# Turns and numerators of a linear-attention front as pairs of 64-row matmuls, with the front's order made anew

## The chip, the cores and the metric

The kernel runs on one core of a Trainium2 chip. A core has five engines with an instruction queue each: TensorE (PE, matmuls into PSUM; its weight loads are shown as PEld), VectorE (DVE), ScalarE (ACT), GpSimd (POOL) and SyncE (SP). Each works through its queue in order. Transfers between HBM and the on-chip SBUF go over 16 DMA engines; SP and POOL issue them here, and each of the two has a DMA queue of its own. The metric is device microseconds of one execution, as the median of several runs. A matmul takes a stationary operand (`lhsT`, up to 128 rows by 128 columns) and a moving one (`rhs`); a turn (transpose) is a matmul with an identity matrix.

## The reference

A linear attention over 8 batches, 8 heads, 576 tokens, head size 64, followed by a mixture of 8 experts with Sinkhorn-normalised gates:

```python
q_p, k_p = (phi(q), phi(k))              # phi(x) = (x if x > 0 else exp(x) - 1) + 1
kv = np.einsum('bhsd,bhse->bhde', k_p, v)
z = np.sum(k_p, axis=2)
num = np.einsum('bhsd,bhde->bhse', q_p, kv)
den = np.einsum('bhsd,bhd->bhs', q_p, z)[..., None] + 1e-06
x = num / den                            # then laid out as (4608 tokens, 512)
logits = x @ w_gate; P = exp(logits - max); 8 rounds of row and column normalisation
for e in range(8):
    out += P[:, e:e + 1] * (np.maximum(x @ w1[e], 0.0) @ w2[e])
```

## The kernel before

**Stages.** The front makes `xT`, the attention output with features on the partitions, in fp16. The experts follow: hidden activations `h`, then outputs `ye`, gated and added into `acc`. For expert 0 the first five groups of 512 tokens are plain matmuls (hidden: L626, 32 matmuls of 128x512 a group; output: L894, 32 of them); they are the work with which TensorE fills the front. Later units use a seven-product scheme, with sums of `x`, of weights and of `h` made on DVE. Sinkhorn runs on DVE behind the front.

**A block of the front** is `att(b, g)`: one batch and four heads, 16 blocks numbered n = 2b + g. Heads stand in two pairs: `hh` picks the 64 partitions on which a head of a pair lies, `r` the pair. Tokens of a batch are split as partition w (64) and j (9). The steps of a block, with the profile's lines:

- loads of k, q and v (L293), by SP for blocks 0, 1 and 6 to 15, by POOL for blocks 2 to 5 and for v from block 6 on (then with a cast to fp16). k and q share a tile `kqin` of which there are two, so k of block n + 2 waits for the last reader of k and q of block n;
- ACT: exp of k and of q (L309); DVE: `t` = max(x + 1, 1) (L322), then min with exp (L325), for k and q each; v is copied into `vv` (L260 on DVE, L258 on ACT), beside a column of ones;
- TensorE L354: k'v and k's sum over the 9 values of j, as 18 matmuls with a contraction of 64 rows each, in pairs (`hh` = 0 and 1) that lie on the two halves of the array and write two PSUM banks;
- `kvz` (L368 on DVE, L366 on ACT): the result goes to SBUF in fp16, multiplied by a mask (`diag` or `half_`) that leaves only the blocks of one head each;
- TensorE L384: 9 turns of q, 128x128 each, both heads of a pair at once; copied to `qpT` (L260, L258);
- TensorE L410: numerators and denominators, 10 matmuls of 128 rows with 130 moving columns: 6 and then 4. The mask in `kvz` lets one matmul do two heads;
- denominators plus 1e-6 (L422 on DVE, L420 on ACT), reciprocal (L425), product `xn` (L434 on DVE, L431 on ACT);
- TensorE L449: 10 turns of x, 128x128 each; copied to `xT` (L260, L258).

`logits(b2)` (L470) is 36 matmuls of 8 columns for two batches. At the start TensorE runs 34 warm-up matmuls (L544) between its first tasks.

**Order.** `_Plan` collects tasks with engines, durations and dependences. `order`, a list of task numbers by engine at the end of the kernel, fixes the sequence in which each engine's tasks are emitted, and so its queue. An engine that waits for one task holds up all that stand behind it in its list. In the list of the DMA engines a number stands only for a landing; the transfers themselves move in the order of the queue that issued them.

**Weights.** `load_w1` and `load_w2` issue the expert's weights on POOL (L243), for expert 0 in two parts each. The first part of w1 waits for the gate copy (L345), which waits for v of block 0. POOL's list of before begins: identity, gate copy, w1 part 1 and 2, k, q, v of block 2, k, q, v of block 3, w2 part 1 and 2, k and q of block 4.

DVE's list of before has, at the same place: the `xT` copies of block 0, the denominators, reciprocals and `xn` of block 1, its `xT` copy, and then L322 for k and q of block 2.

Of the kernel before, what the change touches and what calls it, by code (L numbers as in the profile page):

```python
# [10 lines left out]
FP32 = mybir.dt.float32  # L11
FP16 = mybir.dt.float16
# [127 lines left out]
def kernel(  # L140
# [64 lines left out]
    diag = fp.tile([P, 2, D + 1], FP16, tag="diag", name="diag", bufs=1)  # L205
    half_ = fp.tile([P, 2], FP32, tag="half", name="half", bufs=1)
    p_kv = S_.pool(2)

    def bank_tile():
        return hqp.tile([P, 1024], FP16, tag="hq", name="hq")  # L210

# [63 lines left out]
    def att(b, g):  # L275
# [82 lines left out]
        tkv = fadd(("pe", 0.54), f_kv, deps=[tph["k"], *tvv, *kv_id[n - 1:n], *(num_id[n - 2] if n > 1 else [])], acq=[gkv],  # L358
                   use=[gvv, gt["k"]], prio=pr)

        def f_z(e):
            gz["tile"] = fp.tile([P, 2, 2, D + 1], FP16, tag="kvz", name="kvz")
            kv_ = gkv["tile"][:, :, 0:2 * (D + 1)].rearrange("p h (r d) -> p h r d", r=2)
            if e == "act":
                for r in range(2):
                    nc.scalar.mul(out=gz["tile"][:, :, r, :], in_=kv_[:, :, r, :], mul=half_[:, r:r + 1])  # L366
            else:
                nc.vector.tensor_tensor(out=gz["tile"], in0=kv_,  # L368
                                        in1=diag[:, None, :, :].broadcast_to([P, 2, 2, D + 1]), op=ALU.mult)
        tz = [fadd({"dve": 0.42, "act": 0.63}, f_z, deps=[tkv], acq=[gz], use=[gkv], prio=pr)]  # L370
# [6 lines left out]
        for j0, j1 in ((0, 5), (5, NJ)) if n < 2 else ((0, NJ),):  # L377
            gp = S_.grp(p_hq if n < 2 else p_kv)

            def f_qt(_, gp=gp, j0=j0, j1=j1):  # L380
                tl = bank_tile() if n < 2 else pair_tile(FP16).rearrange("p b t -> p (b t)")
                gp["tile"] = tl[:, 0:(j1 - j0) * 2 * PW].rearrange("p (j h w) -> p j h w", h=2, w=PW)
                for j in range(j0, j1):
                    nc.tensor.transpose(gp["tile"][:, j - j0].rearrange("p h w -> p (h w)"),  # L384
                                        gt["q"]["tile"][:, j, 2:4, :].rearrange("p r d -> p (r d)"), ident)

            def f_qc(e, gp=gp, j0=j0, j1=j1):
                copy(e, gq["tile"][:, :, j0:j1, :].rearrange("p h j w -> p j h w"), gp["tile"])
            t1 = fadd(("pe", 0.058 * (j1 - j0)), f_qt, deps=[tph["q"], tqa, t_init], acq=[gp], use=[gt["q"]], prio=pr)
            tq.append(fadd({"act": 0.165 + 0.105 * (j1 - j0), "dve": 0.14 + 0.069 * (j1 - j0)}, f_qc, deps=[t1, tqa],  # L390
                           use=[gp, gq], prio=pr))
# [4 lines left out]
        def f_xa(_):  # L396
            gxn["tile"] = fp.tile([P, 5, 2, 2, D], FP16, tag="xn", name="xn")
# [3 lines left out]
        for i0, i1 in ((0, 3), (3, 5)):  # L401
# [3 lines left out]
            def f_num(_, i0=i0, i1=i1, gn=gn, grd=grd):  # L405
                gn["tile"] = pair_tile()
                grd["tile"] = fp.tile([P, 2, 6], FP32, tag="rden", name="rden", bufs=4)
                for i in range(i0, i1):
                    for hh in range(2):
                        nc.tensor.matmul(gn["tile"][:, hh, 2 * D1 * (i - i0):2 * D1 * (i - i0 + 1)],  # L410
                                         lhsT=gq["tile"][:, hh, js[i]:js[i] + 2, :].rearrange("p j w -> p (j w)"),
                                         rhs=gz["tile"][:, hh].rearrange("p r e -> p (r e)"), start=True, stop=True)

            def num(gn=gn, ni=ni):
                return gn["tile"][:, :, 0:2 * D1 * ni].rearrange("p h (m e) -> p h m e", e=D1)
# [11 lines left out]
            def f_xn(eng, num=num, grd=grd, i0=i0, i1=i1, ni=ni):  # L427
                if eng == "act":
                    for m in range(2 * ni):
                        for h in range(2):  # L430
                            nc.scalar.mul(out=gxn["tile"][:, i0 + m // 2, m % 2, h, :], in_=num()[:, h, m, 0:D],  # L431
                                          mul=grd["tile"][:, h, m:m + 1])
                    return
                nc.vector.tensor_tensor(  # L434
                    out=gxn["tile"][:, i0:i1].rearrange("p i r h e -> p h (i r) e"), in0=num()[:, :, :, 0:D],
                    in1=grd["tile"][:, :, 0:2 * ni, None].broadcast_to([P, 2, 2 * ni, D]), op=ALU.mult)
            t1 = fadd(("pe", 0.12 * ni), f_num, deps=tq + tz + [txa], acq=[gn, grd], use=[gq, gz], prio=pr)
# [4 lines left out]
        for c0, c1 in ((0, 1), (1, 2)) if n < 2 else ((0, 2),):  # L442
            gx = S_.grp(p_hq if n == 0 else p_kv)

            def f_xt(_, gx=gx, c0=c0, c1=c1):
                gx["tile"] = bank_tile()[:, None, :] if n == 0 else pair_tile(FP16)[:, 0:c1 - c0]
                for c2 in range(c0, c1):
                    for i in range(5):
                        nc.tensor.transpose(gx["tile"][:, c2 - c0, 64 * js[i]:64 * js[i] + P],  # L449
                                            gxn["tile"][:, i, c2].rearrange("p h e -> p (h e)"), ident)  # L450

            def f_xc(e, gx=gx, c0=c0, c1=c1):
                copy(e, xT[:, 2 * g + c0:2 * g + c1, S * b:S * b + S], gx["tile"][:, :, 0:S])
            t1 = fadd(("pe", 0.28 * (c1 - c0)), f_xt, deps=txn, acq=[gx], use=[gxn], prio=pr)
            t1 = fadd({"act": 0.11 + 0.53 * (c1 - c0), "dve": 0.04 + 0.42 * (c1 - c0)}, f_xc, deps=[t1], use=[gx], prio=pr)
            for c2 in range(c0, c1):
                xt_done[(b, 2 * g + c2)] = t1
# [5 lines left out]
    def logits(b2):  # L463
# [11 lines left out]
        t1 = lg_pe[b2] = fadd(("pe", 1.0), f_l, deps=[xt_done[(b, c)] for b in (2 * b2, 2 * b2 + 1) for c in range(NDT)],  # L475
# [78 lines left out]
    nc.vector.memset(diag, 0.0)  # L554
    nc.vector.memset(half_, 0.0)
    for i in range(2):
        nc.vector.memset(vv_t[i][:, :, :, D], 1.0)
        nc.vector.memset(diag[64 * i:64 * i + 64, i, :], 1.0)
        nc.vector.memset(half_[64 * i:64 * i + 64, i:i + 1], 1.0)
# [43 lines left out]
    def layer1(e, g):  # L603
        gw1, tw1, gw2, tw2 = w_t[e]
        bs = range(512 * g // S, (512 * g + 511) // S + 1)
        xd_ = [xt_done[(b, c)] for b in bs for c in range(NDT)]
# [10 lines left out]
        for f, c0, c1 in jobs:  # L617
# [13 lines left out]
            t1 = add(("pe", 0.2175 * (c1 - c0)), f_hq, deps=[tw1[f // 4], prev_hq[0]] + xd_[0:c1 if g == 0 else None],  # L631
# [9 lines left out]
    def x_blocks(g):  # L641
        bs = range(512 * g // S, (512 * g + 511) // S + 1)
        deps = [xt_done[(b, c)] for b in bs for c in range(NDT)]
# [205 lines left out]
    def out_dma(g, tt, deps, c0=0, cw=DM):  # L849
        def f_o(_):  # L850
            for half in range(2):
                bb, j = divmod(2 * (4 * g + tt) + half, NJ)
                dst = AP(tensor=out.tensor, offset=(S * bb + j) * DM + c0, ap=[[NJ * DM, PW], [1, cw]])
# [276 lines left out]
    for d, k_ in zip(chain, chain[1:]):  # L1130
# [3 lines left out]
        pool 0 50 106 108 110 112 114 140 142 144 171 173 177 179 544 181 207 209 211 241 271 303 333 363 393 425 455  # L1134
        485 515 525 576 573 1561 1081 1570 1563 1572 1574 1565 1109 1107 1083 1567 1230 1206 1576 1204 1232 1327 1329
        1353 1355
        pe 2 3 4 5 6 7 8 9 10 11 12 13 14 15 16 17 18 56 54 19 51 20 21 22 63 59 23 24 25 88 90 26 27 85 28 29 67 69
        97 93 614 615 30 616 31 32 33 101 103 34 35 617 618 620 622 624 626 127 628 124 630 632 134 157 154 130 164
        638 636 160 138 637 639 168 640 641 651 653 194 191 634 175 197 655 635 224 657 221 201 659 227 661 663 231
        673 665 205 251 671 254 235 674 672 284 261 684 281 686 688 257 291 690 667 287 668 265 692 669 295 316 694  # L1140
        313 346 670 343 297 323 696 353 700 349 698 319 717 706 719 376 701 373 721 327 357 723 707 403 383 725 379
        702 727 406 729 438 704 387 435 705 409 413 731 703 750 441 752 417 739 445 733 465 740 498 495 734 468 501
        735 505 754 449 756 509 758 471 737 419 475 738 529 526 760 479 532 762 536 764 736 540 770 771 542 768 571
        769 766 794 808 810 796 798 767 800 802 814 772 804 816 818 812 806 547 773 846 820 848 852 850 860 854 826
        856 550 864 866 862 827 858 868 828 898 829 553 904 902 870 900 822 823 556 824 872 908 825 906 912 880 559
        914 916 910 918 878 881 920 922 950 876 562 956 952 879 924 954 874 875 958 877 960 964 565 926 970 962 966
        968 974 1014 1016 972 976 1020 928 1022 1018 1024 929 927 1026 1028 568 1030 932 1034 1036 1032 930 1038 1042
        1044 931 1040 1048 1050 1046 933 1052 982 980 1054 1056 981 1058 1062 983 1064 1060 1066 1137 1139 978 1068
        1143 984 979 985 1145 1141 1074 1076 1079 1147 1084 1087 1149 1151 1153 1090 1157 1159 1155 1161 1165 1167
# [77 lines left out]
```

## Time and profile before

| what | value |
|---|---|
| median of 3 runs | 954.46 us (953.85 to 954.76) |
| the profiled execution's span | 952.4 us |
| TensorE | 943.2 us busy in 7092 matmuls, clock 1.00 |
| front (L470 of the last two batches) | ends near 121.8 us |
| loads of k, q by SP | 576 KB each |
| weight loads of POOL | 512 KB in SBUF for a half of expert 0's w1 or w2 |

How to read it: the span runs from the first to the last instruction; the median of the runs is taken around the whole execution. Times in the trace count from the span's start. A group "x18" is a merged row of 18 instructions. A matmul's own duration (219 ns for a 128-column turn) is its passage through the array; the next one starts earlier, and what a matmul costs is the distance from start to start (56 ns there).

### The profile page before, as it was taken

The page shows a single profiled execution, that of the slowest core. Times are in us where ns is not written, and L with a number is a line of the kernel's source. Part 1 is how long each engine was busy: PE and PEld are TensorE (multiplying, and loading weights), DVE is VectorE, ACT ScalarE, POOL GpSimd, SP SyncE. Part 2 cuts the span into 40 slices and gives each one's busy share as a digit, 9 for nine tenths or more (in the row PEclk, how much of TensorE's full clock was granted, in tenths as well). Part 3 has the DMA queues.
Part 4 walks back from the last instruction along what each step waited for, and adds up shares of the span by engine and source line. Part 5 has one row for each costly group of instructions (what it writes and reads, how often), then busy time and mean ns, then how long its engine had stood idle before and what let it go on. Part 6 is the DMA issues. An engine that isn't in the chain of part 4 may idle for free.

```text
span 952.4 us, 18434 instructions
## 1 busy us (share of the span) xinstructions
PE 943.2 (99%) x7092; PEld 643.9 (68%) x7092; DVE 771.0 (81%) x1527; ACT 566.6 (59%) x1030; POOL 161.5 (17%) x209
## 2 busy tenths in 40 slices
PE   8999999999999999999999999999999999999998
PEld 4566676466676667766676666766676666766676
DVE  6999998788887787888887787887877788877776
ACT  6799755665555555555555555555555555555551
POOL 4210100012122211221112211221112211111111
PEclk9999999999999999999999999999999999999999
DMA  9989983253255422544145431644125431425545
GB/s 310 326 247 255 217 251 115 48 98 89 67 150 112 111 67 61 112 111 100 57 128 116 93 96 43 137 111 101 57 73 105 110 95 56 139 78 151 153 113 133
DMA packets 109944, 118.85 MB, mean 125 GB/s; under 512 B 7840, under 2 KB 95520, under 8 KB 109856
## 3 DMA queue, kind: packets, MB, share of 16 engines
q1 hardware_dynamic: 81600, 90.33, 31.1%
q0 software_dynamic: 27856, 26.82, 16.5%
q8 instruction: 55, 0.90, 0.4%
q10 hardware_dynamic: 400, 0.52, 0.2%
q14 instruction: 33, 0.27, 0.1%
HBM read 119.69 MB, written 17.69 MB: 144 GB/s over the span
## 4 chain that ended last, share of the span: by engine, by line
PE 96%; DMA 2%; DVE 1%; SPq 0%; ACT 0%; POOL 0%; issue 0%; POOLq 0%
PE ye L1032 34%; PE hq L772 20%; PE att L772 10%; PE ye L894 7%; PE Zye L1032 6%; PE Zye L772 5%; PE hq L777 4%; PE hq L626 3%; PE att L777 2%; DMA kqin<-in_k_dram 2%; PE Zye L777 1%; PE kv_ps L354 1%; PE kv_ps L449 1%; PE kv_ps L410 1%; PE kv_ps L384 1%; PE kv_ps L470 0%
## 5 line engine op out<-in xcount | busy, mean ns | idle before, releaser
L1046 DVE SCALAR_TENSOR_TENSOR acc<-ye,P_sb,acc 128x256 f32<-128x256 f32 x620 | 266.8, 476 | 103.7 <-PE ye L1032 101.6
L1032 PEld LDWEIGHTS <-S 128*128 128x128 f16 x1984 | 194.1, 98 | 45.9 <-issue 0.2
L1056 POOL TENSOR_TENSOR acc<-acc,h 128x256 f32<-128x256 f32 x124 | 103.0, 848 | 603.3 <-ACT h L1053 603.3
L1032 PE MATMUL ye<-h,S 128*128 128x256 f16 x1488 | 192.8, 273 | 0.0
L1032 PEld LDWEIGHTS <-h 128*128 128x128 f16 x1488 | 145.6, 98 | 39.9
L812 ACT ACTIVATE h<-hq 128x512 f16<-128x512 f32 x134 | 80.1, 598 | 136.3 <-PE hq L772 117.6
L772 PEld LDWEIGHTS <-W 128*128 128x128 f16 x896 | 87.7, 98 | 81.0 <-issue 0.2
L772 PE MATMUL hq<-xs,W 128*128 128x512 f16 x448 | 133.2, 379 | 0.0
L772 PE MATMUL att<-xs,W 128*128 128x512 f16 x448 | 133.2, 379 | 0.0
L772 PE MATMUL hq<-xs,w 128*128 128x512 f16 x448 | 124.1, 379 | 0.0
L772 PEld LDWEIGHTS <-w 128*128 128x128 f16 x672 | 65.8, 98 | 54.8
L815 DVE CUSTOM_DVE_ANT_0 h<-att,s 128x512 f16<-128x512 f32 x126 | 86.4, 685 | 20.3 <-ACT s L799 19.9
L809 ACT ACTIVATE h<-Zye 128x512 f16<-128x512 f32 x134 | 80.2, 599 | 31.8 <-PE Zye L772 27.3
L1053 ACT ACTIVATE h<-Zye,P_sb 128x256 f32<-128x256 f32 x124 | 52.5, 471 | 77.7 <-PE Zye L1032 75.6
L792 ACT COPY Zye<-hq 128x512 f32<-128x512 f32 x134 | 77.7, 580 | 31.7 <-PE hq L772 25.0
L815 DVE CUSTOM_DVE_ANT_0 h<-hq,s 128x512 f16<-128x512 f32 x126 | 86.3, 685 | 12.4 <-PE hq L772 11.8
L799 ACT COPY s<-hq 128x512 f32<-128x512 f32 x126 | 73.6, 584 | 34.2 <-PE hq L772 29.9
L1003 DVE TENSOR_TENSOR S<-h 128x1024 f16<-128x1024 f16 x124 | 85.0, 685 | 5.5 <-ACT h L812 5.5
L806 ACT COPY s<-att 128x512 f32<-128x512 f32 x126 | 74.5, 591 | 1.2 <-PE hq L777 0.7
L894 PE MATMUL ye<-w,h 128*128 128x512 f16 x296 | 73.7, 379 | 0.0
L772 PE MATMUL Zye<-xs,w 128*128 128x512 f16 x224 | 66.6, 379 | 0.0
L1032 PE MATMUL ye<-w,h 128*128 128x256 f16 x496 | 64.3, 273 | 0.0
(129 smaller groups left out, 1078.3 us busy)
## 6 DMA issues: line engine op xcount, KB each, us to landing
xs<-xd SPq DMA_DIRECT2D x196, 256.0 KB, 4.1
w<-in_moe_w_dram POOLq DMA_DIRECT2D x48, 256.0 KB, 4.2
out_dram<-acc SPq DMA_DIRECT2D x67, 128.0 KB, 2.4
kqin<-in_k_dram SPq DMA_DIRECT2D x12, 576.0 KB, 4.3
kqin<-in_q_dram SPq DMA_DIRECT2D x12, 576.0 KB, 6.1
xs<-xd SPq DMA_DIRECT2D x49, 128.0 KB, 2.3
xd<-xT SPq DMA_DIRECT2D x27, 128.0 KB, 3.8
vin<-in_v_dram POOLq DMA_DIRECT2D x10, 288.0 KB, 5.9
```

The lines of the kernel that those rows point to most:

```text
L772: nc.tensor.matmul(dst, lhsT=lhs(0, c), rhs=X(b)(c), start=(first and c == 0), stop=(c == 1), skip_group_check=True)
L792: nc.scalar.copy(out=Zt[1], in_=gX["tile"])
L799: nc.scalar.copy(out=gs2["tile"], in_=gX["tile"])
L806: nc.scalar.copy(out=gs5["tile"], in_=gR["tile"])
L809: nc.scalar.activation(out=hd(0, 0), in_=Zt[1], func=AF.Relu)
L812: nc.scalar.activation(out=hd(1, 0), in_=gX["tile"], func=AF.Relu)
L815: nc.vector._custom_dve(TENSOR_ADD_SAT, out=dst, in0=ps, in1=sb, s0=3.0e38, s1=0.0)
L894: nc.tensor.matmul(gy[tt]["tile"], lhsT=hx(f, P * tt, P), rhs=gw2["tile"][:, f, :], start=(f == 0), stop=(f == NFT - 1))
L1003: nc.vector.tensor_tensor(out=gS[i]["tile"], in0=a0, in1=a1, op=op)
L1032: nc.tensor.matmul(bank(g_)[:, s, :], lhsT=lhs(s, kk), rhs=rhs(kk), start=(new and s == 0 and kk == 0), stop=(kk == 3), skip_group_check=True)
L1046: nc.vector.scalar_tensor_tensor(out=dst(), in0=bank(g_)[:, s, :], scalar=P_sb[:, gg, e:e + 1], in1=dst(), op0=ALU.mult, op1=ALU.add)
L1056: nc.gpsimd.tensor_tensor(out=dst(), in0=dst(), in1=gst["tile"], op=ALU.add)
```

## The change

- q is turned by 18 matmuls of 64 rows (`turn`), one for each head, in pairs on the halves of the array. The two halves write two PSUM banks, so that each bank holds one `hh`. The copies to `qpT` are cut by bank for blocks 0 and 1.
- The numerators of the two heads of a pair are matmuls of 64 rows and 65 columns, again as pairs on two banks: 20 for a block in place of 10. So the mask in `kvz` falls away, with `diag`, `half_` and their memsets; `kvz` becomes a plain copy.
- x is turned by 18 matmuls of 64 rows; the even and the odd j of a batch go to two banks, and the copies to `xT` are cut into one of 2 x 256 and one of 2 x 320 columns. The tokens of a batch stand in another order in `xT` (j = 0, 2, 4, 6 and then 1, 3, 5, 7, 8), and `out_dma` maps the output rows accordingly.
- The dependences follow (two copies behind each `xT` part), the plan's durations too, and every list in `order` is replaced.

```diff
+    def turn(dst, src, h):
+        r_ = slice(64 * h, 64 * h + 64)
+        nc.tensor.transpose(dst, src[r_], ident[r_, r_])
...
-            kv_ = gkv["tile"][:, :, 0:2 * (D + 1)].rearrange("p h (r d) -> p h r d", r=2)
-            if e == "act":
-                for r in range(2):
-                    nc.scalar.mul(out=gz["tile"][:, :, r, :], in_=kv_[:, :, r, :], mul=half_[:, r:r + 1])
-            else:
-                nc.vector.tensor_tensor(out=gz["tile"], in0=kv_,
-                                        in1=diag[:, None, :, :].broadcast_to([P, 2, 2, D + 1]), op=ALU.mult)
+            copy(e, gz["tile"].rearrange("p h r d -> p h (r d)"), gkv["tile"][:, :, 0:2 * (D + 1)])
...
-                for j in range(j0, j1):
-                    nc.tensor.transpose(gp["tile"][:, j - j0].rearrange("p h w -> p (h w)"),
-                                        gt["q"]["tile"][:, j, 2:4, :].rearrange("p r d -> p (r d)"), ident)
+            for j in range(NJ):
+                for hh in range(2):
+                    turn(tl[hh][:, PW * j:PW * j + PW], gt["q"]["tile"][:, j, 2:4, :].rearrange("p r d -> p (r d)"), hh)
...
-                        nc.tensor.matmul(gn["tile"][:, hh, 2 * D1 * (i - i0):2 * D1 * (i - i0 + 1)],
-                                         lhsT=gq["tile"][:, hh, js[i]:js[i] + 2, :].rearrange("p j w -> p (j w)"),
-                                         rhs=gz["tile"][:, hh].rearrange("p r e -> p (r e)"), start=True, stop=True)
+                        for r in range(2):
+                            s = slice(64 * r, 64 * r + 64)
+                            m = 2 * (i - i0) + hh
+                            nc.tensor.matmul(gn["tile"][:, r, D1 * m:D1 * m + D1],
+                                             lhsT=gq["tile"][s, hh, js[i]:js[i] + 2, :].rearrange("p j w -> p (j w)"),
+                                             rhs=gz["tile"][s, hh, r, :], start=True, stop=True)
...
+            for c2 in range(2):
+                for i in range(5):
+                    for s in range(1 if i == 4 else 0, 2):
+                        o = 320 * c2 + PW * i
+                        turn(tl[s][:, o:o + PW], gxn["tile"][:, c2, i].rearrange("p h e -> p (h e)"), s)
...
+                j = (0, 2, 4, 6, 1, 3, 5, 7, 8)[j]
```

The task numbers in the new `order` shift with the number of tasks. Read back into names, the lists begin so (a dot and the block):

```
POOL  identity, w2 part 1, gate copy, w2 part 2, w1 part 1, w1 part 2, k.2, q.2, v.2, k.3, q.3, v.3, k.4, q.4, v.4, k.5, w_gate, ...
DVE   t_k.0, vv.0, min_k.0, t_q.0, t_k.1, min_q.0, t_q.1, kvz.0, qpT.0 (two), vv.1, min_k.1, ...,
      xn.0 (two), min_q.1, qpT.1 (two), t_k.2, min_k.2, t_q.2, recip.1, xT.0, add.1, recip.1, xT.0, xn.1, min_q.2,
      xT.1 (two), t_k.3, min_k.3, kvz.2, qpT.2, vv.3, t_q.3, kvz.3, min_q.3, ...
PE    ..., L354.0, ..., L384.0, ..., L410.0 (two), ..., L354.1, L384.1, ..., L449.0, L410.1, two warm-ups, L626 of group 0 (two halves),
      L449.1, L384.2, L626, warm-up, L354.2, L626 (four halves), L354.3, L410.2 (two), L626, ...
```

In the new PE list bursts of 64-row matmuls (L354 and the three that the change makes) often stand side by side, as L384.4 L354.4, or L449.3 L449.2. POOL's list of before had w2 behind v.3.

## The prediction

> **What bounds the kernel now.** I read the page first: busy times, then the slices.
>
> ```profile
> span 952.4 us, 18434 instructions
> PE 943.2 (99%) x7092; PEld 643.9 (68%) x7092; DVE 771.0 (81%) x1527; ACT 566.6 (59%) x1030; POOL 161.5 (17%) x209
> ...
> DVE  6999998788887787888887787887877788877776
> ...
> DMA  9989983253255422544145431644125431425545
> ```
>
> TensorE is busy 99%, so a microsecond off its work is a microsecond off the time, as long as it never waits. DVE and the DMA engines are full only in the first slices (23.8 us each): the attention front. The busy times of stretches of it:
>
> ```profile
> 0.00:31.00 31.00, 25.97 (x227) 13.90 (x227) 21.89 (x51) 22.54 (x35) 14.50 (x24) 1.00 1.03 300
> 31.00:60.00 29.00, 29.00 (x307) 17.51 (x306) 26.70 (x50) 22.34 (x32) 3.31 (x5) 1.00 1.02 315
> ...
> 90.00:122.00 32.00, 32.00 (x377) 20.32 (x375) 29.58 (x60) 22.15 (x41) 2.48 (x4) 1.00 0.99 226
> ```
>
> (PE, weight loads, DVE, ACT, POOL; clock, DMA share, GB/s.) TensorE has no gap from 31 us on; before 31 us it has gaps, and part of its work is warm-up. There the transfers set the pace: DMA share 1.03. So two prices count: the work in the packed part, and the time at which it begins.
>
> **Prices on TensorE**, from the chain of waits around 40 us (start, length, what):
>
> ```profile
> 39.72 0.50 PE kv_ps L384 x9
> 40.22 0.62 PE kv_ps L354 x18
> 40.84 0.97 PE ye L894 x4
> 41.81 0.88 PE kv_ps L470 x36
> 42.70 0.36 PE kv_ps L410 x6
> 43.06 0.86 PE hq L626 x4
> ```
>
> Nine turns of q cost 0.50, six numerators 0.35 (four 0.23), ten turns of x 0.56: 1.64 us a block (one batch, four heads). L354 is already what the change makes of the others: 64-row pairs on two banks. Its two matmuls start 3 to 4 ns apart, the next pair 57.4 ns on, so a pair costs what one full matmul of 130 columns does. At 64 columns: 512 columns take 215.7 ns and 128 take 56, so 0.416 ns a column, and 64 take 29.4; I take 30 a pair. Bounds: 25, the 8-column matmuls of L470 (0.88/36), and 50, two of these in turn. The pair of L354 is nearest. New block: q 9 pairs 0.27, numerators 10 pairs 0.30, x 8 pairs and 2 singles 0.30; **0.77 us less a block**.
>
> The Trainium skill (TensorE: Matmul & The Clock Gate, the section on 56 ns) says that starts never fall below about 25 ns however few the columns. L470 agrees (24.6), L354 does not, its pair being 3 to 4 ns apart. By the rule a pair would cost 50 and the gain would nearly vanish; that is the third rival below.
>
> A change of mode costs too. Nine pairs at 57.4 are 0.52, the burst takes 0.62: 0.10 going in; the 512-column group behind it takes 0.97, not 0.86: 0.11 coming out. **0.21 a run** of 64-row bursts; neighbours share it. Before there are 16 runs (L354 alone). In the new PE order I count 80 bursts in 43 runs.
>
> **The start.** The new lists also move things. On POOL's queue the load of w2 (two issues) moves from behind v of block 3 to the front: first part before the gate copy, second right behind it, both ahead of w1 and of the k, q, v of blocks 2 and 3. That queue is served in its order, and the transfers are full:
>
> ```profile
> 2.00:11.00 9.00, 8.00 (x47) 3.28 (x45) 4.53 (x7) 4.64 (x6) 2.62 (x4) 1.00 1.02 376
> 11.00:16.50 5.50, 4.42 (x62) 3.10 (x62) 4.61 (x10) 4.54 (x9) 5.19 (x7) 1.00 1.19 198
> 16.50:25.30 8.80, 7.90 (x56) 4.13 (x53) 6.39 (x14) 7.24 (x17) 3.01 (x4) 1.00 1.04 392
> 25.30:31.00 5.70, 5.00 (x68) 3.10 (x66) 5.39 (x12) 4.85 (x7) 2.98 (x5) 1.00 1.21 236
> ```
>
> 2 to 11 us are SP's six loads of blocks 0 and 1, then w1 (5.5 us), the six loads of blocks 2 and 3, then w2 (5.7 us). With w2 in front those six land 5.7 later, unless POOL leaves the DMA engines idle: w2's first half shares the engines with SP's loads from 3.6 us (issue 1.3; w1's issue at 8.81 began to move at 11.02), these end near 13.9, and the second half's packets come at 13.6, behind the gate on v of block 0 (8.35 before, some 2.6 later). So no idle.
>
> ```profile
> 19.66 0.46 DVE L260 COPY xT<-kv_ps 128x576 f16<-128x576 f16 x1 [1.27 <-PE kv_ps L449]
> 20.04 0.75 DVE L322 TENSOR_SCALAR t<-kqin 128x1152 f16<-128x1152 f32 x1
> 21.58 0.76 DVE L322 TENSOR_SCALAR t<-kqin 128x1152 f16<-128x1152 f32 x1 [0.79 <-DMA kqin<-in_q_dram]
> ...
> 24.59 0.76 DVE L322 TENSOR_SCALAR t<-kqin 128x1152 f16<-128x1152 f32 x1 [0.25 <-DMA kqin<-in_k_dram]
> ```
>
> Before, DVE copies xT of block 1 and only then takes up k and q of block 2 (19.93, 21.58) and k of block 3 (24.57). These become 25.6, 27.3 and 30.3. And the new DVE list puts both L322 of block 2 ahead of the xT copies of block 0 and of block 1's reciprocals. So xT of batch 0, which the first expert matmuls (L626) need, waits for q of block 2. DVE from 27.3: L322 0.75, reciprocal 0.20, copy 0.42, add and reciprocal 0.36, copy 0.49: 29.5. **L626 starts near 29.6, not 16.75.** On: numerators of block 1 0.96, L325 0.72, two copies 0.91, L322 and L325 of block 3 1.47, kvz 0.42, qpT 0.75, vv of block 3 0.75: 35.5, and TensorE's L354 of block 3 near **36.0, against 29.67** (with 0.5 for DVE's waits on TensorE). L354 of block 2 (ACT: 1.75, 1.16, 1.15 behind 28.3, so 32.4) is earlier. What else queues behind those L322 is block 1's, late but not on the path. Block 0's vv copy, now ahead of its L325, costs 4 us there, hidden: block 1's DVE work that precedes L322 ends near 22.
>
> From L354 of block 3 TensorE's order is long enough to be packed. Against before at this point:
> - later: 6.3
> - still to do, done by then before: 18 of the 32 L626 of group 0, 3.9; four numerators and q of block 3, 0.7
> - less: 12 blocks at 0.77 (9.25), and of blocks 2 and 3 the numerators 0.56, x 0.52, one q 0.23: **10.55**
> - more: 35 runs against 13, 22 at 0.21: **4.6**
>
> Sum 6.3 + 3.9 + 0.7 - 10.55 + 4.6 = **+5.0**. Two things I add 1.0 for. DVE: 5.4 of its 84.9 us between L322 of block 4 (35.55) and the last xT copy (120.43) are idle; the new list starts there near 46 with about 1 us less work, so it ends between 124.6 (no idle) and 130 (the same), while TensorE reaches the last logits near 127.7: 0 to 2.3. And TensorE waits some 6 us ahead of 29.6. No gap before is so long, so its price is bounded by 0 and by the 20 or so matmuls behind it at the 427 ns of the first warm-ups in place of 216, most of it beside DVE's chain: 0 to 2. The Trainium skill (TensorE: Matmul & The Clock Gate, Part 1) says that an idle window of about 3.4 us halves the clock; no row here can show it, and by it the sum would stand 1 higher at most.
>
> At nothing: the memsets of diag and half_ (1.3 to 1.9 us, before k lands at 4.7; without that cover 0.5); kvz as a plain copy and the xT and qpT copies cut otherwise (by the lists DVE loses about 1 us in the front, ACT gains 2 at 73 of 91 busy; uncovered it would be that 1); the output rows' new order, as many transfers; the lists behind the front, where TensorE stays packed.
>
> Profile 952.4 + 6.0 = 958.4; the median stands 2.06 above the span, so **960.5**. Own range 956.5 to 967: ACT or DVE earlier by 3, or all that I added at its upper ends.
>
> **Rivals.**
> 1. Faster, 948.5: the first 31 us absorb w2, since TensorE's time there is padding. Then only -10.55 + 4.6 = -5.95 is left. For it: 34 warm-ups. Against it: share 1.02 to 1.21 leaves the transfers no room, and DVE's list waits for q of block 2 by name.
> 2. No change, 955.3: w2's first half slips between SP's packets (1.19 and 198 GB/s show that w packets move few bytes), the delay halves to 2.8, and half the switches hide in waits (2.3): 6.0 - 2.9 - 2.3 = +0.8. Needs both.
> 3. Slower still, 967.7: pairs at 50 ns. The gain of a block falls to 0.24, 10.55 to 3.3, so +7.25. For it: L470. Against it: L354.
>
> **Numbers.** Forecast 0.70, rival 1 0.16, rival 2 0.06, rival 3 (with a TensorE that runs dry behind the front) 0.08. A difference within 0.2% (1.9 us) can't be told from none. Faster 0.16, same 0.06, slower 0.78. The range leaves out about a tenth at each end: 951.5 to 967; it takes in part of rival 1.
>
> **What would show it.** First L626-type matmul near 29.6; L322 of block 2 waiting for DMA until 25 to 27; L354 of block 3 near 36; pairs 30 ns apart; 43 runs at 0.21; last logits near 128, no gaps behind. Wrong if L626 starts before 22, or if w2's packets lie behind k of block 2.

## The result, and the profile after

| | before | after |
|---|---|---|
| median of 4 runs | 954.22 us (953.85 to 954.76) | 963.22 us (962.84 to 963.95) |
| ratio to before, 95% interval | | 1.0095 (1.0081 to 1.011) |
| span of the profiled execution | 952.4 us | 961.0 us |

The changed kernel is slower by 9.0 us; 960.5 was forecast, within 951.5 to 967. The lines of the program have moved: L626 of before is L637, L354 is L356, L410 is L414, L894 is L906, L470 is L485, L322 and L325 are L324 and L327, L434 is L438, the copies L260 and L258 are L262 (DVE) and L260 (ACT). All turns, of q and of x, now have the one line of the helper `turn`, L212; the operand tells them apart (`t` for q, `xn` for x).

First the page of the changed kernel: busy times, then slices of 24.0 us in tenths.

```profile
span 961.0 us, 19274 instructions
PE 940.3 (98%) x7524; PEld 632.1 (66%) x7524; DVE 768.8 (80%) x1525; ACT 567.3 (59%) x1032; POOL 161.5 (17%) x209
...
DVE  4799988679897787887877788877878788877776
...
PEclk8899999999999999999999999999999999999999
DMA  9789928655235431644125431644215441425545
```

TensorE's busy time went from 943.2 to 940.3 although it issues 432 matmuls more. The span grew because TensorE no longer works all the time: DVE's first digit fell from 6 to 4, and the clock has an 8 in the first two slices, where it had none before. The same stretches that the prediction quoted (columns: PE, weight loads, DVE, ACT, POOL; clock, DMA share, GB/s):

```profile
2.00:11.00 9.00, 5.31 (x17) 1.89 (x15) 1.99 (x3) 2.34 (x3) 1.53 (x3) 1.00 1.02 297
11.00:16.50 5.50, 3.17 (x41) 1.55 (x41) 4.27 (x9) 2.33 (x2) 5.04 (x8) 0.60 1.13 318
16.50:25.30 8.80, 6.22 (x105) 2.85 (x104) 4.62 (x10) 0.64 (x2) 1.49 (x2) 0.86 1.17 278
25.30:31.00 5.70, 1.63 (x4) 0.43 (x4) 4.76 (x10) 5.20 (x12) 1.41 (x2) 0.54 1.04 394
```

The DMA share is over 1 throughout, as before, so what is put in front of a queue should delay what stands behind it by its whole length. Who is late by that is seen in the timeline of DVE (start, length, instruction, and in brackets the idle time before it and what ended it):

```profile
25.45 0.76 DVE L324 TENSOR_SCALAR t<-kqin 128x1152 f16<-128x1152 f32 x1 [4.27 <-DMA kqin<-in_k_dram]
...
27.38 0.75 DVE L324 TENSOR_SCALAR t<-kqin 128x1152 f16<-128x1152 f32 x1
...
28.17 0.37 DVE L262 COPY xT<-hq 128x512 f16<-128x512 f16 x1
...
28.80 0.43 DVE L262 COPY xT<-hq 128x640 f16<-128x640 f16 x1
```

DVE stands idle for 4.27 us until k of block 2 has landed; q of block 2 is taken up at 27.38 (21.58 before), and only behind it come the two copies of `xT` of block 0, at 28.17 and 28.80. The chain of waits shows what hangs on the second copy, and how the front goes on:

```profile
28.88 0.36 DVE xT L262
29.23 0.14 issue
29.37 1.86 PE hq L637 x4
31.23 0.66 PE kv_ps L212 x20
31.90 0.02 issue
31.92 0.82 DVE xT L262 x2
...
34.27 0.34 DVE kvz L262
34.61 0.66 DVE qpT L262
35.27 0.68 DVE vv L262
35.95 0.05 issue
36.00 0.71 PE kv_ps L356 x18
...
39.84 0.37 PE kv_ps L212 x18
40.21 1.83 PE hq L637 x8
42.04 0.41 PE kv_ps L414 x20
```

The first expert matmuls start at 29.37 (16.75 before), L356 of block 3 at 36.00 (29.67). Right behind the gap of 5.77 us, four L637 take 1.86 and the turn of x 0.66, at a clock of 0.54; run 7 shows what they take without the gap. The last lines give the new prices: a burst of nine q pairs is 0.37 long, with the way into the 64-row mode; twenty numerators are 0.41.

TensorE's waits from 28 us to the last logits (who waits, for what, us in total, times, the longest):

```profile
PE hq L637 <- DVE xT L262: 5.8, 1, 5.8
PE kv_ps L414 <- DVE kvz L262: 0.4, 1, 0.4
PE kv_ps L356 <- DVE xn L438: 0.3, 1, 0.3
PE kv_ps L356 <- DVE vv L262: 0.3, 1, 0.3
```

The first line is the late start. The others are short, as are the two that the view shows behind the last logits (0.4 each); that the waits grew in number and sum against before is told by the account that follows.

**Where the 8.6 us of span came from.** I added up the distances between the starts of neighbouring matmuls by what they belong to, from L356 of block 3 (L354 of before) to the end of the last logits, and behind it. For an ordinary matmul the distance beyond its usual one counts as waiting; at a change of mode up to 0.10 us of it counts as the change.

| us | before | after | difference |
|---|---|---|---|
| start of L356 of block 3 | 29.67 | 36.00 | +6.33 |
| first hidden layer (L637) | 27.64 | 31.77 | +4.13 |
| output matmuls (L906), to the last logits and behind them | 29.39 + 34.52 | 31.22 + 32.80 | +0.11 |
| numerators, q, x | 7.94 + 6.04 + 7.83 | 4.68 + 3.64 + 4.28 | -9.21 |
| changes of mode (25, 69) | 2.34 | 6.52 | +4.18 |
| waits up to the last logits | 0.39 | 2.02 | +1.63 |
| waits behind them | 0.82 | 1.98 | +1.16 |
| the rest | | | +0.3 |

The rows sum to 8.6, the difference of the spans. How much of a small excess counts as a wait and how much as a burst's own time is a choice: with one fixed price for each kind of matmul the bursts come to -9.6, the waits up to the last logits to +2.3, and the other rows stay within 0.3.

### The profile page after: what moved, and what is told of

Its sections match the earlier page's. It is cut to its first block, busy times and chain, and to the rows that moved or that the text cites. A ratio compares the mean times of both kernels' runs of the same rounds, so it can differ in the third digit from the quotient of the medians.

```text
span 961.0 us, 19274 instructions
## 1 busy us (share of the span) xinstructions
PE 940.3 (98%) x7524; PEld 632.1 (66%) x7524; DVE 768.8 (80%) x1525; ACT 567.3 (59%) x1032; POOL 161.5 (17%) x209
## 4 chain that ended last, share of the span: by engine, by line
PE 92%; DVE 3%; DMA 2%; ACT 1%; issue 0%; SPq 0%; POOL 0%; DVEq 0%; ACTq 0%
PE ye L1044 34%; PE hq L783 20%; PE att L783 10%; PE Zye L1044 6%; PE ye L906 5%; PE Zye L783 5%; PE hq L788 4%; PE hq L637 3%; PE att L788 2%; DMA kqin<-in_k_dram 1%; PE Zye L788 1%; DMA vin<-in_v_dram 1%; PE kv_ps L212 1%; PE kv_ps L356 1%; DVE xn L438 0%; DVE xT L262 0%
## 5 line engine op out<-in xcount | busy, mean ns | idle before, releaser
L906 PE MATMUL ye<-w,h 128*128 128x512 f16 x296 | 73.0, 379 | 0.0
L1044 PE MATMUL ye<-w,S 128*128 128x256 f16 x496 | 64.3, 273 | 0.4 <-DVE acc L1058 0.4
```

The source lines that it names most:

```text
L906: nc.tensor.matmul(gy[tt]["tile"], lhsT=hx(f, P * tt, P), rhs=gw2["tile"][:, f, :], start=(f == 0), stop=(f == NFT - 1))
L1044: nc.tensor.matmul(bank(g_)[:, s, :], lhsT=lhs(s, kk), rhs=rhs(kk), start=(new and s == 0 and kk == 0), stop=(kk == 3), skip_group_check=True)
```

## The experiments

My theory: the pairs do what they should, the changes of mode take half of that, and the rest of the loss is the new order of the first 36 us, with w2 in front of the queue. Rival: the order is harmless or it is DVE's list, not POOL's, that costs the time. Each kernel was timed beside the kernel before on the same chip, in several rounds; "before" is 953.8 to 954.2 us in all of them. Block numbers stand behind a dot.

**1. w2 back behind v of block 3.** Only POOL's list of the changed kernel:

```diff
- pool identity, w2 part 1, gate copy, w2 part 2, w1 (two), k.2, q.2, v.2, k.3, q.3, v.3, k.4
+ pool identity, gate copy, w1 (two), k.2, q.2, v.2, k.3, q.3, v.3, w2 part 1, w2 part 2, k.4
```

> The changed kernel with w2's two loads put back behind v of block 3 in POOL's list; nothing else. Theory (the packed part begins late because w2 holds up k, q and v of blocks 2 and 3 by 5.7 us): L324 for q of block 2 near 21.6 in place of 27.4, the first L637 near 24, L356 of block 3 near 30.3 in place of 36.0, time 963.2 - 5.7 = 957.5. Rival (the loss is made by the changes of mode and the waits of the 64-row bursts in the packed part): the start moves, the time stays near 963. Rival (DVE's list alone holds the start): L356 of block 3 stays near 36.

Measured 957.25 us (956.32 to 958.69), 1.0033 (1.0021 to 1.0045) of before: 6.0 less than the changed kernel. DVE's timeline in this kernel:

```profile
18.79 0.76 DVE L324 TENSOR_SCALAR t<-kqin 128x1152 f16<-128x1152 f32 x1 [0.69 <-DMA kqin<-in_k_dram]
...
20.72 0.75 DVE L324 TENSOR_SCALAR t<-kqin 128x1152 f16<-128x1152 f32 x1
```

k and q of block 2 are taken up 6.7 us earlier than with w2 in front (25.45 and 27.38); L637 starts at 22.71 and L356 of block 3 at 29.20, 6.8 earlier; 1.0 of that goes into waits behind it, one of 1.2 at 87 us above all. The place of two issues on one queue is two thirds of the slowdown.

**2. DVE's copies of `xT` ahead of k and q of block 2**, w2 still in front:

```diff
- dve t_k.2, min_k.2, t_q.2, recip.1, xT.0, add.1, recip.1, xT.0, xn.1, min_q.2, xT.1 (two)
+ dve recip.1, xT.0, add.1, recip.1, xT.0, xn.1, xT.1 (two), t_k.2, min_k.2, t_q.2, min_q.2
- act exp_k.2, add.1, exp_q.2, xn.1
+ act add.1, xn.1, exp_k.2, exp_q.2
```

> The changed kernel with w2 still first, but in DVE's list the xT copies, the reciprocals and xn of block 1 ahead of L324 for k and q of block 2, and in ACT's list the denominators and xn of block 1 ahead of exp of block 2. Theory: L637 then starts when w1 has landed, 21 to 24, and L356 of block 3 falls to about 33.3, since k of block 3 still lands at 30: time near 960.5. If DVE's list is the whole cause, L356 of block 3 near 29 and 956; if it costs nothing, 963.

Measured 965.30 (964.29 to 966.09), 1.0117 (1.0102 to 1.0132): slower than the changed kernel by 2.1, where I had expected 2.7 less. **3. Both edits together:**

> Both edits: w2 behind v of block 3, and block 1's DVE and ACT work ahead of block 2's. Theory: L637 at 17 to 21, L356 of block 3 near 28.4, that is 7.6 before the changed kernel's, time near 955.6; it stays above the kernel before because TensorE's list still puts 18 matmuls of group 0 (3.9 us) behind L356 of block 3. If the two delays add up wholly (5.7 and 2.7), 954.8. Rival (modes and waits): 963.

Measured 960.47 (960.23 to 960.86), 1.0067 (1.0052 to 1.0082): 3.2 slower than edit 1 alone. Both moves put all of block 1's work ahead of L324 of block 2. In the third kernel that work holds up L324, as DVE's timeline shows:

```profile
22.85 0.82 DVE L262 COPY xT<-kv_ps 128x512 f16<-128x512 f16 x2 [0.75 <-PE kv_ps L212]
23.59 0.75 DVE L324 TENSOR_SCALAR t<-kqin 128x1152 f16<-128x1152 f32 x1
```

K of block 2 had landed at 19.15, but L324 came at 23.59 (18.79 in kernel 1). Two thirds of the 4.4 us between are DVE's work on blocks 0 and 1, the rest are waits of 0.81 and 0.75 for the turns of x of these blocks. The second of these turns stands in TensorE's list behind two halves of L637, which themselves wait for DVE.

In the second kernel that cost little: k of block 2 landed at 26.16 there, and L324 came at 26.51. In both, however, the turn of q of block 2, which in kernel 1 follows the turn of x without a gap, now waits 4 us for DVE's work on block 2, and what TensorE does behind that gap runs at a lowered clock. TensorE in the second kernel, then in the third:

```profile
33.02 1.16 PE L356 MATMUL kv_ps<-vv,t 64*128 64x130 f16 x18 [1.17 <-ACT vv L260]
34.11 3.60 PE L637 MATMUL hq<-xT,w 128*128 128x512 f16 x8
```

```profile
26.79 0.66 PE L212 MATMUL kv_ps<-ident,t 64*128 64x64 f16 x18 [3.98 <-DVE t L327]
...
29.87 2.54 PE L637 MATMUL hq<-xT,w 128*128 128x512 f16 x8
```

Eight L637 take 1.90 in kernel 1. From L356 of block 2 to L356 of block 3 it is 2.55 us there, 3.56 in the third kernel and 4.62 in the second, where the granted clock is 0.50 from 30 to 37.6 us. In the second kernel nothing is won up to L356 of block 2, which starts as in the changed kernel (33.02 and 33.16), since ACT's copy of v behind the exp of block 3 releases it; behind it the clock puts L356 of block 3 at 37.64 in place of 36.00. In the third, L356 of block 3 comes at 32.34 in place of 29.20; by the usual distances of its matmuls about 2 of these 3.1 us are the clock's. So DVE's order was not the mistake of the changed kernel: as long as TensorE's list stays as it is, it is the better one.

**4. w2 in front, in the kernel before.** This tells the place of w2 from everything else:

```diff
- pool identity, gate copy, w1 (two), k.2, q.2, v.2, k.3, q.3, v.3, w2 (two)
+ pool identity, w2 part 1, gate copy, w2 part 2, w1 (two), k.2, q.2, v.2, k.3, q.3, v.3
```

> The kernel before with only w2's two loads moved to the front of POOL's list, as the change has them. Theory: k and q of block 2 land 5.7 later, L354 of block 3 goes from 29.67 to about 35.4, L626 of group 0 are still all done by then, so the time is 954.2 + 5.7 = 959.9. Rival (the start is padding and absorbs w2): 954 to 955.

Measured 959.60 (959.52 to 961.15), 1.0063 (1.0046 to 1.008): 5.6 slower than before. The timeline of DVE, to be held against the lines at 20.04 and 21.58 in the prediction:

```profile
25.42 0.76 DVE L322 TENSOR_SCALAR t<-kqin 128x1152 f16<-128x1152 f32 x1 [0.94 <-DMA kqin<-in_k_dram]
26.91 0.76 DVE L322 TENSOR_SCALAR t<-kqin 128x1152 f16<-128x1152 f32 x1 [0.74 <-DMA kqin<-in_q_dram]
```

5.3 to 5.4 us later, as L354 of block 3 is (35.00). Undone in the one kernel w2's place is worth 6.0, done in the other 5.6; it does not depend on the pairs.

**5. The start of before.** With w2 back, the lists of TensorE, DVE and ACT for blocks 0 to 3 and the hidden layer of group 0 put as in the kernel before (with it five more tasks on ACT and five fewer on DVE); from there on as changed. The hidden layer of group 0, of which 4.1 us lay behind the start, is done in the front again.

> The changed kernel with the lists of POOL, TensorE, DVE and ACT for blocks 0 to 3 and group 0 put in the order that they have in the kernel before; pairs, copies and the lists from block 4 on as changed. Theory (the change loses at its start and gains by its pairs): L356 of block 3 near 29.7 with all 32 matmuls of group 0 done; left are the pairs (about -9.6 on the blocks behind), the changes of mode (+4.5) and the waits of the changed lists (+1.6 to 2.8): time 954.0 - 2.3 to 3.5 = 951, the fastest of all. Rival (the 64-row runs cost more than they save): 954 or more.

Measured 956.07 (954.80 to 957.05), 1.002 (1.0011 to 1.0029): 5 above what I expected. L356 of block 3 started at 29.54 as hoped, but TensorE then waited. Its timeline:

```profile
38.86 1.05 PE L485 MATMUL kv_ps<-wg_sb,xT 128*128 128x8 f16 x36 [2.19 <-DMA wg_sb<-in_moe_w_gate_dram]
...
40.70 3.51 PE L906 MATMUL ye<-w,h 128*128 128x512 f16 x8
```

The changed lists issue w_gate behind k of block 5, and the first logits, now earlier, met it. Behind this wait eight L906 took 3.51, where the eight at 33.41 took 1.90: the lowered clock, 1.5 us more. The two make 3.7 of the 5.

**6. The halves one after the other.** Kernel 5 with the loops of each burst exchanged, so that the 64-row matmuls of q, x and numerators are issued one half after the other:

```diff
-            for j in range(NJ):
-                for hh in range(2):
+            for hh in range(2):
+                for j in range(NJ):
                     turn(...)
...
-                for i in range(i0, i1):
-                    for hh in range(2):
-                        for r in range(2):
+                for r in range(2):
+                    for i in range(i0, i1):
+                        for hh in range(2):
...
-            for c2 in range(2):
-                for i in range(5):
-                    for s in range(1 if i == 4 else 0, 2):
+            for s in range(2):
+                for c2 in range(2):
+                    for i in range(4 + s):
```

> The same start, but each burst issues all matmuls of one half of the array first and then all of the other, so that neighbours share a half and a bank; the same matmuls, the same changes of mode. Theory (two halves side by side make the gain): a matmul then costs 25 to 29 on its own, a pair 50 to 58 in place of 29; bursts of q 0.45 to 0.5 in place of 0.27; for blocks 4 to 15 and parts of 2 and 3 some 350 pairs at 21 to 27 more, +7 to +9.5: 958 to 961. Rival (pairing buys nothing, only fewer columns do): 951.

Measured 959.12 (957.49 to 959.40), 1.005 (1.0037 to 1.0064): 3.05 slower than kernel 5. One burst of x in each (kernel 5, then this one):

```profile
35.24 0.47 PE L212 MATMUL kv_ps<-ident,xn 64*128 64x64 f16 x18
```

```profile
36.38 0.60 PE L212 MATMUL kv_ps<-ident,xn 64*128 64x64 f16 x18
```

From L356 of block 3 on the bursts grew by 0.93 (numerators), 1.37 (x) and 1.52 (q), 3.8 in all; the start came 1.0 later and the waits were some 1.7 less. But the edit did not do all that it was meant to. Read start by start, the burst of x at 36.38 begins with five matmuls 29 ns apart (39 behind the first) and ends with seven 29 to 30 ns apart; in between the starts lie 8 to 21 ns apart, as two rows of 29 ns each, one for each half. So the second half begins before the first is done, and some of the matmuls still run side by side; the means of 20 (numerators), 22 (x) and 23 ns (q) a matmul come from that. One that goes alone costs 29 ns, as I had put it at most, and two of 64 columns in turn 58, against 56 for one of 128. The 3.8 is then a lower bound for what side by side is worth. My estimate for none at all side by side: the 740 matmuls of the bursts at 29 ns are 21.5 us, what the bursts of the kernel before cost (21.8). By it, fewer columns alone win nothing; no run here shows it directly.

**7. Warm-ups in the gap.** The changed kernel, with two of its warm-up tasks made 14 matmuls long, so that TensorE is not idle for 6 us ahead of L637:

```diff
-    def f_warm(_):
-        nc.tensor.matmul(yw[0], lhsT=warm[:, 0:P], rhs=warm, start=True, stop=True)
+    def f_warm(_, i=0):
+        for _ in range(14 if i in (31, 32) else 1):
+            nc.tensor.matmul(yw[0], lhsT=warm[:, 0:P], rhs=warm, start=True, stop=True)
```

> The changed kernel with the two warm-up tasks ahead of group 0 made 14 matmuls each, so that TensorE stays busy from 23 to 29 us and its clock is not lowered when L637 starts. Theory: the lowered clock delays the x turn of block 1 and DVE's copies of it by about 1.2 us, so L356 of block 3 comes 0.7 to 1.2 earlier: 962.0 to 962.5. Rival (the lowered clock is hidden behind DVE's chain): 963.2. Rival (the lowered clock is what costs): 958 or less.

Measured 962.63 (962.22 to 963.01), 1.0091 (1.0077 to 1.0104). That is 0.6 below the changed kernel's median, but the ranges overlap (962.84 was its fastest), and the spans are 961.1 and 961.0. L356 of block 3 starts at 35.95 in place of 36.00. That does not mean that the clock cost nothing. In the profiled execution k of block 2 landed 1.04 later (L324 at 26.49, not 25.45; in the four kernels with w2 in front it lands between 25.4 and 26.5), and still L356 of block 3 was not late. The chain, to be held against the lines at 29.37 and 31.23 above:

```profile
30.41 1.02 PE hq L638 x4
31.43 0.41 PE kv_ps L212 x18
```

(The lines of the program are one further here.) The clock is 1.00 from 25.3 to 31.0, not 0.54, and the four expert matmuls and the turn of x take 1.43 in place of 2.52; from L324 to L356 of block 3 it is 9.46 in place of 10.55. So the lowered clock takes 1.1 us on the changed kernel's chain, as the theory of this run had it; the late landing hides it in the span. How much of it the median shows, four runs do not tell.

**8. w_gate two issues earlier** in kernel 5, and the first logits four tasks later:

```diff
- pool k.4, q.4, v.4, k.5, w_gate
+ pool k.4, q.4, w_gate, v.4, k.5
```

> e5_start_of_before with w_gate's load two issues earlier in POOL's list (behind q of block 4, as in the kernel before) and the first logits four tasks later in TensorE's list. In e5 the logits waited 2.3 us for w_gate, and eight matmuls behind them ran at half the clock (1.5 us more). Theory: both go, 956.1 - 3.9 = 952.2, faster than the kernel before by 0.1 to 0.3%. If only the wait goes: 953.8. If the wait comes back elsewhere: 956.

Measured 953.48 (953.04 to 955.02), 0.9996 (0.9986 to 1.0005): no difference from before that can be told, 1.3 above what I expected. The 2.2 us are gone, and the slow L906 with them, but by the account above 2.5 us of waits stay ahead of the last logits and 2.5 behind (before: 0.4 and 0.8).

**9. The changed instructions in the whole order of before.** Every list of before is kept, task by task; where a task was split or joined, its parts stand together.

> The changed instructions (pairs, plain kvz copy, cut copies) in the whole order of the kernel before, task for task: 56 runs of 64-row bursts in place of 43, 46 of them from L356 of block 3 on in place of 13. Theory: start as before (L356 of block 3 near 29.5, group 0 done), pairs -9.6, 33 more runs at 0.20 each +6.6, waits +0.5 to 1: 951.3 to 952. Rival (the runs cost more than the pairs save): above 954. Rival (the changed lists from block 4 on are themselves better than the old ones): e8 faster than this by 2 or more.

Measured 951.93 (951.29 to 953.17), 0.9978 (0.9969 to 0.9987): **the fastest of all, 2.2 us below before and 11.3 below the changed kernel**. Its busy times and TensorE's waits, for the stretches that were packed before:

```profile
31.00:60.00 29.00, 29.00 (x412) 14.90 (x411) 27.55 (x53) 23.17 (x36) 3.24 (x5) 1.00 1.03 316
...
90.00:122.00 32.00, 31.93 (x482) 16.47 (x477) 30.11 (x66) 20.08 (x37) 2.48 (x4) 1.00 1.00 225
```

```profile
PE kv_ps L356 <- DVE xn L438: 0.7, 1, 0.7
PE kv_ps L414 <- DVE kvz L262: 0.3, 1, 0.3
PE kv_ps L212 <- DVE t L327: 0.2, 1, 0.2
```

The first of these waits lies ahead of L356 of block 3, where the account begins. By the same account as above: bursts -9.53, changes of mode +6.43 (93 in place of 25), waits +0.2; with some 0.6 in the rest this gives the spans' -2.3. This is the worth of the pairs without a new order.

**10 and 11. Fewer changes of mode.** If 93 changes cost 8.8 us, bursts put side by side should win some back. In kernel 9, bursts that stood alone with one expert task between them were joined, in one kernel by issuing the first of the two later, in the other by issuing the second earlier; for example:

```diff
 10:
- pe q turn.5, L637, L356.5
+ pe L637, q turn.5, L356.5
 11:
- pe q turn.5, L637, L356.5
+ pe q turn.5, L356.5, L637
```

> The kernel with the order of before for all its tasks (e9) has 46 runs of 64-row bursts on TensorE from L356 of block 3 on. Here eleven bursts that stood alone are issued one expert task (0.87 us) later, so that they join the next burst; 36 runs are left. Nothing else moves. If the change of mode costs what I read from the trace (0.096 in, 0.098 and 0.011 out), ten runs fewer are worth 2.0 us: 949.9, with TensorE's waits up to the last logits staying near the 0.56 of e9. Rival: a burst that is 0.87 later makes DVE and then TensorE wait, and waits take the gain back: 951.5 to 952.5, with waits of 2 us or more.

> The same joining, but the second burst of each pair is issued one expert task earlier instead (fourteen places, also 36 runs). Mode changes alone: 949.9. Rival: a burst that is 0.87 us earlier finds its operands not ready, and the expert matmuls that would have covered it stand behind it: each such place costs up to 0.87, so 951 to 955, with these waits named at the numerators and turns in the trace.

Measured 955.62 (955.34 to 956.12), 1.0016 (1.0007 to 1.0025), and 954.07 (953.37 to 955.36), 1.0001 (0.9992 to 1.0009). Both are slower than kernel 9, the first by more than the rival had said. The two theories add up rather than exclude each other: the changes of mode fell from 93 to 71 and from 8.77 to 6.70 and 6.68 us, the 2.1 that their price says; and the waits up to the last logits rose from 0.56 to 5.90 and 5.37. (The eleventh's profiled execution was the slowest of its eleven, 1.3 above their median, so its waits are on the high side.) TensorE's waits in the eleventh; the second line, ahead of L356 of block 3, is there in kernel 9 too:

```profile
PE kv_ps L212 <- DVE xn L438: 1.5, 3, 0.7
PE kv_ps L356 <- DVE xn L438: 0.7, 1, 0.7
PE kv_ps L414 <- DVE xn L438: 0.6, 1, 0.6
PE kv_ps L356 <- ACT vv L260: 0.5, 1, 0.5
```

Bursts of neighbouring steps wait for DVE's and ACT's work in between, `xn` above all, which both gives the turn of x its operand and gives back the numerators' PSUM tile, of which there are two (`kv_ps`). The expert task between two bursts had been the time in which DVE did this; with DVE at 27.55 of 29 us, no other such time is left.

## Why the prediction was right, and where its sizes were off

**The start: right.** L626 (L637) was put at 29.6 and came at 29.37; L354 (L356) of block 3 at 36.0 and came at 36.00. The way there was right as well: w2 delays k and q of block 2, DVE's list puts both ahead of `xT`, and L637 waits for `xT`. That it came out so exactly is luck: 0.5 was put for DVE's waits on TensorE in this stretch, and the one for the turn of x alone is 1.18, as the clock had fallen; L637 came 0.2 earlier and DVE's own work was some 0.5 shorter than put. Runs 1 and 4 show the first cause alone, at 6.0 and 5.6. Rival 1, that the front absorbs w2, is refuted by run 4, and rival 2 too, which halved the delay.

**The matmuls left behind the start: right.** 18 of the 32 of group 0 were put at 3.9, and 0.2 more came.

**The pairs: right, 0.6 too large** (0.3 with fixed prices). Its terms for the bursts were +0.7 and -10.55, so -9.85; it is -9.21. A block saves 0.73 in place of 0.77, and the error lies in the numerators: twenty cost 0.33, not 0.30, and q and x 0.28 and 0.31 against 0.27 and 0.30. The trace speaks against rival 3, 50 ns a pair: nine q pairs are 0.27 us long with the mode already set, 30 a pair. The Trainium skill (TensorE: Matmul & The Clock Gate, the section on 56 ns) puts starts never below about 25 ns; here two starts of a pair lie 3 to 4 ns apart, so for the two halves of the array taken together the measurement decides against it. Within one half it holds: 29 ns in run 6.

**The changes of mode: right.** +4.6 forecast, +4.2 measured, at 0.094 us a change; runs 9 to 11 give the same price with 93 and 71 of them. That the 64-row mode must be entered and left at a price the Trainium skill has too (TensorEngine Tiling (Array Packing), Key Properties: switching the mode drains TensorE); the trace shows the price and not the draining.

**The waits: the term that was mis-sized.** The step was "Two things I add 1.0 for", DVE's lateness (0 to 2.3) and the clock (0 to 2). The clock fell as feared (0.54 in the stretch of the gap); by the chains of run 7 it cost 1.1, and this lies in the start, where the shorter work made up for it. The waits that did come are 1.63 up to the last logits and 1.16 behind them, 2.8 in all. I had also put "the lists behind the front, where TensorE stays packed" at nothing, and there the 1.16 are; the last logits ended at 130.7, where 127.7 was put. Run 9 shows that the waits belong to the new lists and not to the pairs: with the lists of before and the same instructions the waits are 0.56 and 0.83. With 1.8 more here, 0.6 less from the pairs, 0.4 less for the modes, 0.3 more expert work and 0.3 in the rest, the forecast of 6.0 becomes the 8.6 of the span.

**What the experiments add.** Of the 10.9 us of span between the changed kernel and kernel 9, the place of w2 is 5.7, measured in run 1; the start of before (kernel 5) is 0.9 more and the place of w_gate (kernel 8) 3.1; the last 1.2 are 3.6 of waits less the 2.5 by which the new PE list has fewer changes of mode. (By the medians the four steps are 6.0, 1.2, 2.6 and 1.5.) Runs 10 and 11 show what such joining is worth when DVE has no room: less than nothing. What was not tried is a joining that keeps the time between a burst and the next one that needs its result; whether it can beat 951.9 stays open.

## What to carry to other kernels

Where transfers set the pace of a front, place loads by the work that waits for them first: two issues moved to the head of one queue cost 5.6 to 6.0 us here, more than twice what pairing saved after its own costs (2.2). Price smaller matmuls with the change of mode that each run of them pays, and before joining runs to save it, look whether the work between them was the cover for another engine. When a list is reordered, look for new gaps on TensorE too: in runs 2, 3 and 5 some 1.5 to 2 us of a miss of 5 each came from work behind a gap, at half the clock. When a change comes with a new order for everything, run its instructions in the old order once; the difference tells what each of the two is worth.

## What the runs showed that I had not expected

- **The granted clock goes by steps of 3.41 us, and a gap counts by how it lies in them.** In the clock records of all thirteen traces a stretch at one clock is a whole number of 3.41 us long (6.83 or 10.24 in the fronts, 945.49 in the kernel before), and the steps begin at another moment in each execution: the first change to the full clock comes 4.04 to 7.29 us after the span's start. For each step of the first 60 us I counted the share of it in which TensorE streamed columns (0.42 ns each at full clock, as 512 take 216). The clock fell to a half behind each of ten steps with 21 to 35%, and behind none of the 172 with 42% or more; it came back behind steps of 75% or more (at 0.84 ns a column) and not behind those of 69% or less. What the chip itself counts, the traces do not show. Two steps of kernel 5 (PE's busy time, 1.70, takes in each matmul's passage; by columns the first step has 27%; the clock is the third number from the end):

```profile
37.15:40.56 3.41, 1.70 (x40) 1.31 (x41) 3.38 (x6) 2.03 (x2) 0.00 (x0) 1.00 0.81 288
40.56:43.97 3.41, 3.41 (x10) 1.18 (x8) 1.74 (x3) 2.54 (x5) 0.70 (x1) 0.50 0.75 220
```

The gap there is 2.19 us, and 1.71 of it lies in one step. In kernel 9 a gap of 2.20 us from 6.50 on is cut by a step's end at 7.45 and does nothing (67 and 49%). So whether such a gap costs anything looks like chance: of kernel 5's eleven executions four have a mean clock of 1.000 and took 954.80 to 955.05 us, seven have 0.997 or 0.998, as one step at half the clock makes it, and took 955.97 to 957.05. In the changed kernel the gaps of 3.95 and 5.77 us leave steps of 21%, 26% and 0%. The Trainium skill (TensorE: Matmul & The Clock Gate, Part 1) gives an idle window of about 3.4 us that runs freely; the length and the free running agree with the trace, but the step need not be idle: up to 35% of work was not enough.

- **Two 64-row halves keep a pace of their own.** Each starts a matmul of 64 columns every 29 ns, whether the other half works or not, and in run 6 the second half began while the first was still at its last three matmuls.
- **The price of a wait can lie in its place.** Joining eleven or fourteen pairs of bursts, each moved by 0.87 us, raised the waits by 5.3 and 4.8 us in the profiled executions, over twice what it saved; the medians lost 3.7 and 2.1 us against kernel 9.
